# Second MLP product by seven products of halves, blocks of 256 tokens, and a new weight conversion, in a fused attention and MLP kernel

## Chip, cores and metric

One NeuronCore of a Trainium2 chip. The metric is the device time of one execution in microseconds; several executions of each kernel, the median is quoted. Each kernel ran beside the kernel before on the same chip. Ratios are the mean time of one kernel's fast runs over that of the other's fast runs of the same rounds, so they aren't quite the ratio of the quoted medians.

## The reference, cut to what matters

Retention attention (no softmax, a causal decay mask) of 8 batches x 8 heads x 576 tokens x 64, then an MLP on 4608 tokens of 512 features with 2048 hidden ones:

```python
def _attn_ref(q, k, v):
    scores = (1.0 / np.sqrt(D_)) * np.matmul(q, k.transpose(0, 1, 3, 2))
    ...                                    # rel = pos_i - pos_j
    Dmat = np.where(rel >= 0, gamma[:, None, None] ** rel[None, :, :], 0.0)
    return np.matmul(scores * Dmat[None], v).astype(np.float32)

def _moe_ref(x, w_in, w_out, alpha):
    h = x @ w_in                           # 4608x512 @ 512x2048
    g = np.maximum(h, 0.0) + alpha * np.minimum(h, 0.0)
    return (g @ w_out).astype(np.float32)  # 4608x2048 @ 2048x512
```

The two weight matrices arrive as 64-bit floats. The chip has to turn them into fp32 by integer work on their halves ("conversion" below): 32 pieces of 128x512, each a 512 KB load and then seven short operations on three engines (six after the change).

## The kernel before

Sixteen "couples" (4 heads of one batch each) go through attention. MLP units (128 hidden features x 384 tokens) are put between the attention's parts as soon as there are tokens for them. All matmul results of attention go through one ring of three PSUM banks, tag `psa`. The conversion uses SBUF alone:

```python
ps_a = tile_pool(name="ps_a", bufs=3, space=PSUM)
ps_h = tile_pool(name="ps_h", bufs=2, space=PSUM)
ps_o = tile_pool(name="ps_o", bufs=NTC, space=PSUM)      # NTC = 3
...
def load_weights(n):                      # 8 pieces a couple, couples 0 to 3
    ...
    nc.sync.dma_start(raw, src...)        # raw: 3 buffers
    nc.gpsimd.tensor_scalar(a, hi, HI_MAX, -HI_MAX, ALU.min, ALU.max)
    nc.scalar.activation(l, lo, ACTF.Copy, scale=2.0 ** -29)
    nc.scalar.activation(b, a, ACTF.Square)
    nc.vector.scalar_tensor_tensor(out=a, in0=b, scalar=HI_MIN * HI_MIN, in1=a,
                                   op0=ALU.is_ge, op1=ALU.mult)
    nc.vector.tensor_scalar(bi, ai, 3, 0x3FFFFFF8, ALU.logical_shift_left, ALU.bitwise_and)
    nc.vector.scalar_tensor_tensor(out=bi, in0=ai, scalar=-0x40000000, in1=bi,
                                   op0=ALU.bitwise_and, op1=ALU.bitwise_or)
    nc.gpsimd.tensor_tensor(out=dst.bitcast(INT32), in0=bi, in1=l, op=ALU.add)
...
def mlp_out():                            # second product: 3 x 512 columns a unit
    for m in range(NTC):
        nc.tensor.matmul(acc[kb][m], g[:, m * P:(m + 1) * P], w_out[...][:, ..., :], ...)
...
for n, (b, u) in enumerate(couples):      # cut
    qT, kT, rT = transposes(n, b, u, tiles)
    at = scores(n, qT, kT, rT)
    states(n, tiles)
    if b < WB:
        load_weights(WPC)
    values(n, b, u, tiles, qT, rT, at)    # its pv, pvr tiles: tag "psa"
```

The listing's order is the program's order.

## Time and profile before

| | before |
|---|---|
| median | 1243.3 us (1241.19 to 1243.61, 3 runs) |
| span of the profiled run | 1242.7 us |
| nominal TensorE work, by pitch | 1171 us |
| tail after the last matmul | 6 us |
| lost in the first 200 us | 66 us |

"Pitch" is the time from one start to the next. A "pass" is one TensorE record of the trace; an fp32 matmul is two of them. "Lost" is the span less the nominal work and the tail.

The prediction shows the lines that carry this.

### The profile page before, as it was taken

The numbers are of one execution on the slowest core, as the hardware profiler recorded it, in microseconds if no ns is written. First come the engines' busy times: TensorE is split into PE (matmuls) and PEld (weight loads), VectorE is DVE, ScalarE is ACT, GpSimd is POOL, SyncE is SP. The second block draws the span as 40 slices with busy tenths as digits, with TensorE's granted clock in tenths as the row PEclk, the third lists the DMA queues.
The fourth block names the chain that finished last, engine by engine and source line by source line (L and its number), as shares of the span: only waits on it lengthen the run. The fifth ranks groups of instructions, "written<-read, shape, count | busy, mean of one in ns | idle before, by whom it ended". The sixth has DMA issues, their size and how long they took to land.

```text
span 1242.7 us, 11962 instructions
## 1 busy us (share of the span) xinstructions
PE 1193.1 (96%) x4897; PEld 670.2 (54%) x4897; DVE 417.0 (34%) x831; ACT 108.3 (9%) x197; POOL 195.2 (16%) x328
## 2 busy tenths in 40 slices
PE   6878789999999999999999999999999999999998
PEld 4644445555555565555555655555555556555553
DVE  5778772223223232312312332232232323222221
ACT  1333220000001001001001000100100100000000
POOL 6567680002001010100100101010010000000000
PEclk9879799999999999999999999999999999999999
DMA  6655631002002120100100201010010000000000
GB/s 153 193 152 166 177 85 45 5 1 60 20 1 64 23 55 30 34 20 30 34 20 30 54 17 41 30 37 17 30 35 20 26 0 1 26 0 1 25 1 26
DMA packets 122774, 55.31 MB, mean 45 GB/s; under 512 B 116304, under 2 KB 116320, under 8 KB 122720
## 3 DMA queue, kind: packets, MB, share of 16 engines
q1 hardware_dynamic: 119808, 45.11, 14.4%
q0 software_dynamic: 2912, 9.45, 2.0%
q8 instruction: 38, 0.62, 0.2%
q14 instruction: 16, 0.13, 0.0%
HBM read 45.10 MB, written 9.44 MB: 44 GB/s over the span
## 4 chain that ended last, share of the span: by engine, by line
PE 61%; issue 27%; POOL 6%; DVE 4%; ACT 1%; DMA 1%; SPq 0%; POOLq 0%; ACTq 0%
PE ph L242 26%; PE po L227 26%; PE pt L285 2%; PE ps L302 2%; PE pv L347 2%; POOL w_in L213 2%; POOL qk L269 1%; PE pv L356 1%; POOL wa L201 1%; PE pu L325 1%; DVE at L306 1%; POOL w_out L213 1%; DVE wa L205 1%; ACT wb L204 1%; DVE wb L211 1%
## 5 line engine op out<-in xcount | busy, mean ns | idle before, releaser
L227 PE MATMUL po<-w_out,g 128*128 128x512 f32 x1152 | 532.2, 598 | 13.0 <-DVE g L248 9.3
L242 PE MATMUL ph<-xT,w_in 128*128 128x384 f32 x1536 | 541.5, 493 | 1.8 <-POOL w_in L213 1.8
L242 PEld LDWEIGHTS ph<-xT,w_in 128*128 128x128 f32 x1536 | 288.2, 191 | 225.9 <-issue 76.1
L227 PEld LDWEIGHTS po<-w_out,g 128*128 128x128 f32 x1152 | 220.0, 192 | 249.8 <-issue 187.3
L246 DVE TENSOR_SCALAR neg<-ph,alpha 128x384 f32<-128x384 f32 x192 | 118.5, 617 | 688.4 <-PE ph L242 687.9
L269 POOL TENSOR_TENSOR qk<-qk,tab 128x256 f32<-128x256 f32 x128 | 86.0, 691 | 233.2 <-DMA qk<-in_q_dram 222.8
L248 DVE SCALAR_TENSOR_TENSOR g<-ph,neg 128x384 f32<-128x384 f32 x192 | 106.8, 556 | 6.2
L235 POOL DMA_DIRECT2D out_dram<-osb x36 | 19.9, 553 | 354.2 <-ACT osb L233 353.9
L264 POOL TENSOR_TENSOR qkr<-qkr,tabr 128x256 f32<-128x256 f32 x16 | 9.8, 614 | 410.6 <-DMA qkr<-in_k_dram 284.1
L359 ACT COPY xT<-pv 128x512 f32<-128x512 f32 x32 | 18.5, 584 | 452.2 <-PE pv L356 451.0
L302 PE MATMUL ps<-qT,kT 64*128 64x128 f32 x512 | 48.8, 287 | 7.8 <-DVE at L306 5.6
L306 DVE TENSOR_TENSOR at<-ps,mask 128x512 f32<-128x512 f32 x64 | 41.4, 685 | 38.6 <-PE ps L302 38.6
L302 PEld LDWEIGHTS ps<-qT,kT 64*128 64x128 f32 x512 | 42.6, 190 | 21.5 <-issue 10.5
L233 ACT COPY osb<-po 128x512 f32<-128x512 f32 x36 | 21.1, 585 | 260.3 <-PE po L227 236.5
L285 PE MATMUL pt<-ident,qk 128*128 128x128 f32 x256 | 36.5, 295 | 0.2
L347 PEld LDWEIGHTS pv<-at,vn 128*64 128x64 f32 x512 | 28.6, 140 | 11.0 <-issue 9.1
L280 ACT COPY rT<-ptr 128x256 f32<-128x256 f32 x16 | 6.0, 375 | 324.5 <-PE ptr L279 324.5
L347 PE MATMUL pv<-at,vn 128*64 128x128 f32 x512 | 32.5, 280 | 1.1 <-DVE atr L315 1.1
L285 PEld LDWEIGHTS pt<-ident,qk 128*128 128x128 f32 x256 | 31.0, 151 | 3.8 <-POOL qk L269 1.0
L356 PE MATMUL pv<-qT,sums 128*128 128x128 f32 x192 | 27.8, 290 | 5.3 <-DVE sums L335 4.3
L213 POOL TENSOR_TENSOR w_in<-wb,wl 128x512 int32<-128x512 int32 x16 | 25.1, 1566 | 33.9 <-DVE wb L211 30.4
L211 DVE SCALAR_TENSOR_TENSOR wb<-wa,wb 128x512 int32<-128x512 int32 x32 | 30.0, 939 | 0.4
(55 smaller groups left out, 382.4 us busy)
## 6 DMA issues: line engine op xcount, KB each, us to landing
out_dram<-osb POOLq DMA_DIRECT2D x36, 256.0 KB, 2.4
qk<-in_q_dram SPq DMA_DIRECT2D x64, 128.0 KB, 2.9
qk<-in_k_dram SPq DMA_DIRECT2D x64, 128.0 KB, 3.0
vn<-in_v_dram SPq DMA_DIRECT2D x64, 128.0 KB, 2.7
raw<-in_moe_w_in_dram SPq DMA_DIRECT2D x16, 512.0 KB, 4.6
raw<-in_moe_w_out_dram SPq DMA_DIRECT2D x16, 512.0 KB, 3.5
qkr<-in_q_dram SPq DMA_DIRECT2D x32, 32.0 KB, 2.2
qkr<-in_k_dram SPq DMA_DIRECT2D x32, 32.0 KB, 2.2
```

Source lines behind the costliest of these rows:

```text
L211: nc.vector.scalar_tensor_tensor(out=bi, in0=ai, scalar=-0x40000000, in1=bi, op0=ALU.bitwise_and, op1=ALU.bitwise_or)
L213: nc.gpsimd.tensor_tensor(out=dst.bitcast(INT32), in0=bi, in1=l, op=ALU.add)
L227: nc.tensor.matmul(acc[kb][m], g[:, m * P:(m + 1) * P], w_out[fc // FCQ][:, fc % FCQ, :], start=(fc == 0), stop=(fc == NFC - 1))
L242: nc.tensor.matmul(ph, w_in[fc // FCQ][:, cc, f0:f0 + P], xT[grp][:, cc, t0:t0 + TB], start=(cc == 0), stop=(cc == NCC - 1))
L246: nc.vector.tensor_scalar(neg, ph, 0.0, alpha[:, fc:fc + 1], ALU.min, ALU.mult)
L248: nc.vector.scalar_tensor_tensor(out=g, in0=ph, scalar=0.0, in1=neg, op0=ALU.max, op1=ALU.add)
L269: nc.gpsimd.tensor_tensor(out=qk[:, x, j], in0=qk[:, x, j], in1=tab[:, x, j, 4 * u:4 * u + 4, None].to_broadcast([P, 4, D]), op=ALU.mult)
L285: nc.tensor.transpose(pt[:, j * C:(j + 1) * C], qk[:, x, j, 2 * i:2 * i + 2, :].rearrange("p h d -> p (h d)"), ident)
L302: nc.tensor.matmul(ps[h2][:, cols], kT[i][rows, cols], qT[i][rows, cols], start=True, stop=True)
L306: nc.vector.tensor_tensor(out=a, in0=ps[h2].rearrange("p (j w) -> p j w", w=C), in1=mask[:, None, :].to_broadcast([P, NJ, C]), op=ALU.mult)
L347: nc.tensor.matmul(pv[i][h2 * D:(h2 + 1) * D, j * C:(j + 1) * C], vn[:, j, 2 * i + h2, :], at[2 * i + h2][:, j, :], start=(j == 0), stop=F ...
L356: nc.tensor.matmul(pv[i][:, j * C:(j + 1) * C], sm[:, j - 1, i, :], qT[i][:, j * C:(j + 1) * C], start=False, stop=(j == NJ - 1), skip_gro ...
```

## The change

Its intent is to take one eighth off the second product (Strassen: seven products of halves for eight) and to shorten the weight conversion, so that the MLP starts sooner. A unit is now 256 hidden features x 256 tokens, and a block has seven accumulators of 256 columns in four banks. The conversion of a piece has one VectorE operation less. The intermediate of the two that are left lies in PSUM, with the intent that VectorE and GpSimd needn't lock each other out of the SBUF port (point 4 of the prediction). A stage of weights is one quarter of both matrices, and a unit asks only for its own stage.

The core of the diff (cuts marked `...`; sums of `g`, attention's scaling and the output's adds are left out):

```diff
-    TB = 384
+    TB = 2 * P
 ...
-    ps_h = ctx.enter_context(tc.tile_pool(name="ps_h", bufs=2, space=bass.MemoryType.PSUM))
-    ps_o = ctx.enter_context(tc.tile_pool(name="ps_o", bufs=NTC, space=bass.MemoryType.PSUM))
+    ps_h = ctx.enter_context(tc.tile_pool(name="ps_h", bufs=1, space=bass.MemoryType.PSUM))
+    ps_o = ctx.enter_context(tc.tile_pool(name="ps_o", bufs=1, space=bass.MemoryType.PSUM))
 ...
-    loaded = {0: load_couple(*couples[0]), 1: load_couple(*couples[1])}
+    loaded = {0: load_couple(*couples[0])}
 ...
-    nc.gpsimd.dma_start(a16, moe_alpha.rearrange("(t p) -> t p", p=P))
+    nc.sync.dma_start(a16, moe_alpha.rearrange("(t p) -> t p", p=P))
 ...
-            nc.gpsimd.tensor_scalar(a, hi, HI_MAX, -HI_MAX, ALU.min, ALU.max)
-            nc.scalar.activation(l, lo, ACTF.Copy, scale=2.0 ** -29)
-            nc.scalar.activation(b, a, ACTF.Square)
-            nc.vector.scalar_tensor_tensor(out=a, in0=b, scalar=HI_MIN * HI_MIN, in1=a,
-                                           op0=ALU.is_ge, op1=ALU.mult)
-            nc.vector.tensor_scalar(bi, ai, 3, 0x3FFFFFF8,
-                                    ALU.logical_shift_left, ALU.bitwise_and)
-            nc.vector.scalar_tensor_tensor(out=bi, in0=ai, scalar=-0x40000000, in1=bi,
-                                           op0=ALU.bitwise_and, op1=ALU.bitwise_or)
+        nc.scalar.activation(a, hi, ACTF.Abs)
+        nc.scalar.activation(l, lo, ACTF.Copy, scale=2.0 ** -29)
+        nc.gpsimd.tensor_scalar(a, a, HI_MIN, HI_MAX, ALU.max, ALU.min)
+        c = ps_a.tile([P, DM], INT32, tag="psa", name=f"wc_{at}")
+        nc.vector.tensor_scalar(c, ai, 3, 0x3FFFFFF8,
+                                ALU.logical_shift_left, ALU.bitwise_and)
+        nc.vector.scalar_tensor_tensor(out=bi, in0=flat[:, :, 1], scalar=-0x40000000, in1=c,
+                                       op0=ALU.bitwise_and, op1=ALU.bitwise_or)
 ...
+            for eng, o, x, y in ((nc.vector, 4, 1, 0), (nc.vector, 5, 3, 4),
+                                 (nc.gpsimd, 6, 5, 2), (nc.gpsimd, 1, 3, 1)):
+                eng.tensor_tensor(out=w[:, o], in0=w[:, x], in1=w[:, y], op=ALU.subtract)
 ...
+    PROD = [(0, 0), (2, 2), (5, 5), (6, 1), (4, 4), (7, 3), (3, 6)]
 ...
-        for m in range(NTC):
-            nc.tensor.matmul(acc[kb][m], g[:, m * P:(m + 1) * P], ...)
+        for n, (x, y) in enumerate(PROD):
+            nc.tensor.matmul(acc[kb][n // 2][:, n % 2, :], g[:, x, :], w_out[i][:, y, :], ...)
```

## The prediction

> **What bounds the kernel now.** I read the page first (busy table and 40 slices), then the windows view in stretches, then the chain of waits inside one steady stretch, then the groups by form, and last the timeline of the first 200 us.
>
> ```profile
> PE 1193.1 (96%) x4897; PEld 670.2 (54%) x4897; DVE 417.0 (34%) x831; ACT 108.3 (9%) x197; POOL 195.2 (16%) x328
> ...
> PE   6878789999999999999999999999999999999998
> ...
> PEclk9879799999999999999999999999999999999999
> ```
> TensorE is busy 96% and at full clock everywhere but the first 7 slices.
>
> ```profile
> 50.00:100.00 50.00, 38.57 (x258) 24.56 (x258) 40.95 (x67) 18.14 (x31) 38.52 (x37) 0.83 0.63 175
> 100.00:150.00 50.00, 39.75 (x156) 21.92 (x158) 35.95 (x51) 16.24 (x28) 36.04 (x37) 0.85 0.61 178
> ...
> 400.00:500.00 100.00, 99.89 (x434) 57.34 (x433) 27.97 (x52) 7.52 (x15) 12.15 (x21) 1.00 0.17 42
> ```
> (Columns: stretch, length, busy PE, PEld, DVE, ACT, POOL, clock, DMA share, GB/s.) Two regimes. Up to about 200 us TensorE has gaps and a clock of 0.83 to 0.85, while DVE and POOL are both over 70% busy: they convert the weights. From 200 us on TensorE has no gap and DVE is 28% busy. The same view for 1200 to 1243 us has TensorE busy 36.76 us.
>
> ```profile
> 408.71 1.53 PE pv L356 x12
> ...
> 418.43 2.58 PE po L227 x6
> 421.00 2.58 PE ph L242 x8
> ...
> 443.72 1.14 PE ps L302 x16
> 444.86 0.68 DVE at L306
> ```
> In the steady chain (start, us, what) the first product of one unit (8 passes of 384 columns; each fp32 matmul is two records) takes 2.58 us and the second (6 passes of 512) also 2.58. That is 322 and 430 ns a pass: 0.84 ns per column and nearly no fixed cost. Ends matter little here, as the pitch comes from starts. Between two successive groups the same chain has 52.55 us (398.86 to 451.41) with 8 units of 5.155, so one attention couple costs 52.55 - 41.24 = 11.3 us of TensorE.
>
> So the nominal TensorE time is 192 units x 5.155 = 990 us, plus 16 couples x 11.3 = 181: 1171 us. The span is 1242.7; that last stretch of 43 us leaves a tail of 6 us. The remaining 66 us are lost in the first 200 us.
>
> **What the Trainium skill says.** (1) "TensorE: Matmul & The Clock Gate", section "Wait — 56ns, not 53.3ns?": a warm matmul starts every N / 2.4 GHz + 2.5 ns. The trace has twice the streaming time per fp32 pass: 2 x 384 / 2.4 + 2.5 = 322.5 and 2 x 512 / 2.4 + 2.5 = 429.2, measured 322 and 430. (2) The same page, "LDWEIGHTS (loading the stationary operand)" and "Step-by-step: what each phase is for": a weight load takes about its columns / 1.2 ns and can run under the matmul before it. The trace agrees: the 12 passes of only 128 columns above (pv, first line of the fence), each with its own 128-column load, take 1.53 us, 128 ns each, so loads are no limit above that. (3) "VectorE: DVE Perf Modes", "The TRN2 errata": an fp32 tensor_tensor takes (N + 151) / 0.96 ns. The rows agree: 512 columns 685 ns (691), 128 columns 283 (291). (4) "SBUF — State Buffer", "Who interferes with whom": DVE with two SBUF inputs, or in a two-port mode, and GpSimd lock each other out; DVE with at most one SBUF input, outside those modes, does not.
>
> ```profile
> L205 DVE SCALAR_TENSOR_TENSOR wa<-wb,wa x32: 674/693/1095, 43.9 to 175.6; 128x512 f32<-128x512 f32 x32
> ...
> L209 DVE TENSOR_SCALAR wb<-wa x32: 408/844/1375, 45.1 to 176.9; 128x512 int32<-128x512 int32 x32
> ...
> L201 POOL TENSOR_SCALAR wa<-raw x32: 642/840/1109, 38.2 to 174.0; 128x512 f32<-128x512 f32 x32
> ```
> (min/median/max ns.) The trace fits the lock: each of these has a short form and one 0.4 to 1 us longer.
>
> **The change part by part.**
> *Matmuls.* A unit becomes 256 hidden features x 256 tokens: 16 passes for the first product and 7 products x 2 = 14 for the second, all of 256 columns. A pass: 2 x 256 / 2.4 + 2.5 = 215.8 ns. Unit: 30 x 215.8 = 6.47 us; 18 blocks x 8 units = 144: 932 us. Against 990 this saves 58 us. The gain is all in the second product (495 to 435 us, nearly one eighth); narrower passes give back 3 us. All of it lies on the path, as TensorE has no gap after 200 us.
> *DVE, steady.* Added per unit: the neg row (617 ns at 384 columns) becomes two of 256, 617 - 128 / 0.96 = 484 each; the g row (556 at 384) becomes one of 512, 690; then four sums of 128 columns, 283 each as the atr row: 2.79 us. Per block seven combinations of 256 columns, (256 + 151) / 0.96 = 424, 2.97 us, 0.37 per unit. 3.2 us in 6.47, half busy, so throughput does not bind. Latency: ph has one PSUM bank instead of two. After the first product DVE must read it out in 0.2 (start delay in the timeline, po at 926.36 to neg at 926.56) + 0.97 + 0.69 = 1.86 us, while TensorE works 14 passes = 3.02 us on the previous unit. 1.2 us of slack. The accumulators are single too: at a block's end the readout and the sums of the next unit take DVE about 5.9 us from the moment ph is full, and TensorE comes back to the accumulators after 6.47. Slack 0.6 us; a GpSimd operation that holds the shared port can use it up. I give 4 us in all.
> *Weights.* DVE per piece before: mean rows 814 + 829 + 939 = 2.58 us; after: two operations with PSUM on one side, about 0.7 each, 1.4. GpSimd per piece before 856 and 1513 (means); after, if the lock is gone, the short forms 0.65 + 1.26 = 1.9. Added: four half-size differences per unit, two on each engine (0.6 and 0.42 each). The q/k scaling (128 x 0.69 + 16 x 0.61 = 98 us) becomes q/v in 32 large ones, about the same. Now the order of instructions: conversion starts at about 27 us instead of 38 (one couple's loads, 10.7 us of issuing, no longer stand before it). Each stage of 8 pieces follows one couple on DVE. Stage 0: 8 pieces at 2.3 us after a 4 us fill, to 48. Stage 1: GpSimd 8 x 1.9 + 2.4 + 5.4 = 23 us. Stages 2 and 3: DVE 5.6 (couple) + 11.2 + 1.7 + three units x 2.8 = 27, 28 with some lock. Sum 127, with a 3 us bubble at each of four turns about 139 us, instead of 181. By then TensorE has done 4 couples, transposes of the fifth (2), 7 first and 6 second products: 45 + 2 + 24 + 18 = 89, nearly 90. Lost 139 - 90 = 49 instead of 66.
> *Tail.* Seven adds instead of three copies, most before the last product: still 6 us.
> Sum: 932 + 181 + 49 + 6 + 4 = 1172; I say 1170.
>
> **The rivals.**
> (a) Weight loads bind at 256 columns. The PEld rows show 191 ns means and PEld would be 30 x 191 = 5.7 of 6.47 us. Against: the 128-column passes at 128 ns. If a pass took 235 ns: 4320 x 19 = 83 us back, 1250. I give 4%.
> (b) The single banks make TensorE wait for DVE. For: the small slack at block ends. If each of 18 blocks lost 1.5 us and each unit 0.1: 27 + 14 = 41, 1210. 8%.
> (c) The start gains nothing, because DVE, now also making the unit's four sums, and the shared psa banks stay the limit: 66 lost again, 1189. 20%.
> (d) The start gains fully: no bubbles, all weights by 127 us, 37 lost: about 1160. 25%.
>
> **Range and chances.** The matmul term is firm (two pitches fitted, one in between). The start is worth -12 to +17 around 1170, waits up to +10 commonly. So 1170, range 1150 to 1195. Faster by 2% means under 1218: only (a), or (b) at its worst, miss it. Faster 0.94, within 2% 0.05, slower 0.01.
>
> **What would show it.** Right: in the steady chain ph groups of 16 passes take 3.45 us and po groups of 14 take 3.02; DVE about half busy there; first product row near 497 us and second near 435 by pitch; the last weight conversion near 139 us; the clock slices full from the fifth or sixth on. Wrong: po or ph waiting for DVE on the row of groups (over 10 us in total), a pitch well above 216 ns, DVE's differences and sums stretched far over 0.4 us beside GpSimd, or the last conversion still near 180.

## More of the kernel before

A scheduler orders the instructions of each engine when the program is built; the order in which tiles take the buffers of a ring is the program's.

The waits of TensorE in the first 200 us of the kernel before (who waited, for what, us in total, times, longest):

```profile
PE po L227 <- DVE g L248: 9.3, 4, 2.9
PE aps L163 <- DMA a<-in_moe_alpha_dram: 8.9, 1, 8.9
PE ps L302 <- DVE at L306: 5.6, 2, 4.8
PE pv L356 <- DVE sums L335: 4.3, 4, 1.3
```

No single wait is large, and the values (`pv`) wait for attention's own sums only. The two outer windows of the start (stretch, length, then busy us of PE, PEld, DVE, ACT, POOL, the TensorE clock granted as a share of full speed, DMA share, GB/s):

```profile
0.00:50.00 50.00, 33.87 (x330) 27.65 (x331) 27.70 (x139) 11.88 (x22) 26.60 (x116) 0.93 0.66 162
...
150.00:200.00 50.00, 45.41 (x150) 23.46 (x148) 31.55 (x48) 7.90 (x12) 25.95 (x23) 0.94 0.21 60
```

TensorE gets through 34 us of work in the first 50 us, because attention runs ahead of the weights.

## The result, and the profile after

| | before | after |
|---|---|---|
| median, same rounds | 1243.45 us (4 runs) | 1232.83 us (1232.12 to 1234.44, 4 runs) |
| ratio | | 0.992, 95% interval 0.9903 to 0.9937 |
| span of the profiled run | 1242.7 | 1232.7 |
| nominal TensorE work | 1171 | 932 + 181 = 1113 (units by the pitches below, couples as before) |
| tail | 6 | 5.7 |
| lost in the start (the rest) | 66 | 114 |

The output is correct. The predicted 1170 us, with a range to 1195, was missed by 63 us. The matmuls did save what was foreseen, and the start lost 48 us more than before. First the chain of waits of the changed kernel in a steady stretch (start us, us, what):

```profile
930.41 3.45 PE ph L268 x16
933.87 3.02 PE po L256 x14
936.89 3.45 PE ph L268 x16
940.34 3.02 PE po L256 x14
```

A unit is 3.45 + 3.02 = 6.47 us, to the hundredth as worked out, and the groups follow each other without a gap. The windows view of the changed kernel:

```profile
0.00:50.00 50.00, 9.28 (x93) 8.45 (x95) 24.95 (x124) 13.52 (x21) 33.80 (x103) 0.77 0.69 178
50.00:100.00 50.00, 20.02 (x172) 16.77 (x168) 21.44 (x40) 16.09 (x30) 41.90 (x32) 0.60 0.48 142
100.00:150.00 50.00, 37.97 (x239) 31.22 (x240) 23.98 (x52) 19.48 (x42) 38.56 (x30) 0.80 0.55 148
150.00:200.00 50.00, 40.55 (x255) 33.55 (x254) 31.38 (x61) 11.77 (x25) 31.11 (x24) 0.90 0.33 93
...
500.00:600.00 100.00, 99.89 (x550) 87.19 (x549) 45.25 (x123) 4.60 (x13) 4.57 (x4) 1.00 0.11 29
```

The last line is the steady state: TensorE full, VectorE 45% busy. Above it TensorE is busy 9 us where before it was 34, then 20 us where it was 39. VectorE, feared as the limit, is less busy than before (21 us instead of 41 in the second stretch), while GpSimd is at 42. What TensorE waited for in the first 200 us:

```profile
PE pv L385 <- DVE wb L207: 52.0, 5, 26.0
PE ph L268 <- DVE g L278: 17.1, 4, 6.2
PE aps L164 <- DMA a<-in_moe_alpha_dram: 13.7, 1, 13.7
```

The first line is new, and odd on its face. The values of attention, `pv`, have no use for `wb`, a tile of the weight conversion. What they share is a bank ring. The timeline of TensorE shows the longest of these waits (start, us, what, and in brackets the idle time before it and what ended it):

```profile
22.22 1.15 PE L365 MATMUL pu<-vn,kn 128*64 128x64 f32 x32 [0.16 <-issue]
49.41 1.98 PE L385 MATMUL pv<-at,vn 128*64 128x128 f32 x16 [26.03 <-DVE wb L207]
```

The first couple's scores and states are done at 23 us. Its values come at 49. In the program's order the eight `wc` tiles of the stage take the ring's three buffers before `pv` does, so `pv` gets a bank only when a late `wc` has been read. The chain of waits has the operation that reads the sixth of the eight (start us, us, what):

```profile
48.59 0.69 DVE wb L207
```

The first `pv` starts right after it. The second starts at 55.10 us, after the seventh piece, and `pvr` at 58.74, after the eighth: three buffers, given out in order. The next couple's values wait behind the next stage in the same way (18.4 us at 90.6).

The second cause is in the groups of the conversion (count: min/median/max ns, first and last start us):

```profile
L201 POOL TENSOR_SCALAR wa<-wa x32: 1907/1916/2022, 28.0 to 183.5; 128x512 f32<-128x512 f32 x32
```

```profile
L205 DVE TENSOR_SCALAR wc<-wa x32: 682/695/696, 30.0 to 185.4; 128x512 int32<-128x512 int32 x32
```

```profile
L209 POOL TENSOR_TENSOR w_out<-wb,wl x16: 1260/1272/1320, 45.3 to 187.5; 128x512 int32<-128x512 int32 x16
```

The last two rows look as the PSUM operand was meant to make them: VectorE's runs flat at 0.69 us where before it was 408/844/1375 ns, and GpSimd's add is flat at 1.27 (before, 1257/1441/1711 for the same tile). But GpSimd's clamp takes 1.92 us and never less, against a median of 0.84 before: 61 us in all instead of 27. The last piece's last operation starts at 187.5 us; before, it was 179.9. "The last piece" below is always this start.

### The profile page after: what moved, and what is told of

Its sections match the earlier page's. It is cut to its first block, busy times and chain, and to the rows that moved or that the text cites. A ratio compares the mean times of both kernels' runs of the same rounds, so it can differ in the third digit from the quotient of the medians.

```text
span 1232.7 us, 16093 instructions
## 1 busy us (share of the span) xinstructions
PE 1134.6 (92%) x6529; PEld 984.7 (80%) x6529; DVE 565.1 (46%) x1535; ACT 112.5 (9%) x283; POOL 191.1 (16%) x226
## 4 chain that ended last, share of the span: by engine, by line
PE 86%; POOL 5%; DVE 3%; DMA 2%; SPq 2%; issue 1%; ACT 1%; DVEq 0%; POOLq 0%; ACTq 0%
PE ph L268 40%; PE po L256 34%; POOL wa L201 3%; PE ps L342 3%; PE pv L394 2%; PE pt L324 2%; PE pv L385 2%; DMA raw<-in_moe_w_in_dram 2%; PE pu L365 1%; SPq L76 1%; DVE at L346 1%; POOL w_out L209 1%; SPq L81 1%; PE psr L353 1%; DVE wb L207 1%
## 5 line engine op out<-in xcount | busy, mean ns | idle before, releaser
L268 PE MATMUL ph<-xb,w_in 128*128 128x256 f32 x2304 | 538.7, 385 | 17.1 <-DVE g L278 17.1
L268 PEld LDWEIGHTS ph<-xb,w_in 128*128 128x128 f32 x2304 | 436.1, 192 | 79.9 <-DVE g L278 12.1
L256 PE MATMUL po<-w_out,g 128*128 128x256 f32 x2016 | 458.5, 379 | 0.0
L256 PEld LDWEIGHTS po<-w_out,g 128*128 128x128 f32 x2016 | 383.0, 190 | 52.1
L276 DVE TENSOR_SCALAR neg<-ph,alpha 128x256 f32<-128x256 f32 x288 | 126.3, 479 | 522.5 <-PE ph L268 522.5
L284 DVE TENSOR_TENSOR g<-g 128x128 f32<-128x128 f32 x576 | 156.1, 311 | 8.7
L278 DVE SCALAR_TENSOR_TENSOR g<-ph,neg 128x512 f32<-128x512 f32 x144 | 99.5, 691 | 4.9
L313 POOL TENSOR_TENSOR vn<-vn,tab 128x1024 f32<-128x1024 f32 x16 | 30.4, 1903 | 428.1 <-DMA vn<-in_v_dram 337.7
L313 POOL TENSOR_TENSOR qn<-qn,tab 128x1024 f32<-128x1024 f32 x16 | 30.6, 1913 | 273.4 <-DMA qn<-in_q_dram 240.6
L201 POOL TENSOR_SCALAR wa<-wa 128x512 f32<-128x512 f32 x32 | 61.3, 1920 | 16.9 <-ACT wa L197 16.9
L205 DVE TENSOR_SCALAR wc<-wa 128x512 int32<-128x512 int32 x32 | 21.9, 692 | 42.7 <-POOL wa L201 42.7
```

Of the source, the lines that this page charges most:

```text
L201: nc.gpsimd.tensor_scalar(a, a, HI_MIN, HI_MAX, ALU.max, ALU.min)
L256: nc.tensor.matmul(acc[kb][n // 2][:, n % 2, :], g[:, x, :], w_out[i][:, y, :], start=(i == 0 and n % 2 == 0), stop=(i == NU - 1 and (n % ...
L268: nc.tensor.matmul(ph[:, x, :], w_in[i // UST][:, cc, x, f0:f0 + P], xb[kb][:, cc, :], start=(cc == 0), stop=(cc == NCC - 1))
L276: nc.vector.tensor_scalar(neg[:, x], ph[:, x], 0.0, alpha[:, fc:fc + 1], ALU.min, ALU.mult)
L278: nc.vector.scalar_tensor_tensor(out=g[:, 0:4, :].rearrange("p x t -> p (x t)"), in0=ph.rearrange("p x t -> p (x t)"), scalar=0.0, in1=neg ...
L284: nc.vector.tensor_tensor(out=g[:, o, :], in0=g[:, x, :], in1=g[:, y, :], op=op)
```

## The experiments

Four sets, on five chips, each with the kernel before on the same chip (its medians are 1242.6 to 1244.9 us, so the sets compare to within 2 us). "Loss" is the span of the profiled run (some 2 us under that run's own time) less 1113 and 5.7.

| run | median us | ratio to before, 95% | loss in the start |
|---|---|---|---|
| after | 1232.83 | 0.9903 to 0.9937 | 114 |
| c_in_pso | 1212.19 | 0.9733 to 0.9765 | 92 |
| c_in_sbuf | 1212.03 | 0.9733 to 0.9764 | 91 |
| clamp_forms | 1219.54 | 0.9791 to 0.9820 | 99 |
| plain8 | 1279.08 | 1.0270 to 1.0301 | other pitch |
| clamp_all | 1209.91 | 0.9716 to 0.9745 | 89 |
| clamp_pso | 1187.27 | 0.9534 to 0.9569 | 67 |
| clamp_sbuf | 1188.17 | 0.9537 to 0.9575 | 69 |
| early_w2 | 1211.99 | 0.9731 to 0.9766 | 94 |
| before_swap | 1266.07 | 1.0168 to 1.0198 | kernel before |
| raw4 | 1195.36 | 0.9607 to 0.9638 | 76 |
| raw4_actq | 1192.46 | 0.9581 to 0.9609 | 71 |
| early_w3 | 1192.21 | 0.9577 to 0.9609 | 72 |
| interleave | 1186.63 | 0.9517 to 0.9546 | 67 |
| no_early_units | 1188.07 | 0.9532 to 0.9563 | 67 |
| free_conv (wrong result) | 1148.36 | 0.9215 to 0.9247 | 28 |
| alpha_q | 1187.54 | 0.9532 to 0.9564 | 68 |

### First set: the theories, one at a time

Theory one: the conversion's PSUM tiles in attention's ring hold up the values. Theory two: the clamp's slow form makes each stage long. The rival to both is that the seven products themselves, by their sums and single banks, cost what they save.

**c_in_pso** puts the conversion's tile of the first two stages into the banks of the second product, which are idle then:

```diff
-        c = ps_a.tile([P, DM], INT32, tag="psa", name=f"wc_{at}")
+        if at < 16:
+            c = ps_o.tile([P, DM], INT32, tag=f"pso{at % 4}", name=f"wc_{at}")
+        else:
+            c = ps_a.tile([P, DM], INT32, tag="psa", name=f"wc_{at}")
```

> The changed kernel, but in stages 0 and 1 the PSUM operand of the weight conversion lies in the four banks of the second product, which are idle then, not in the three banks that the attention uses. Theory 1 (the conversion's use of the attention's PSUM ring makes TensorE wait for whole stages): the waits of the pv matmuls for the conversion, 26.0 and 18.4 us in the first two stages, go to under 3 us each, the x blocks of the first couple are copied near 30 us instead of 61, and the last conversion is 10 to 20 us earlier than 187.5: about 1215 us. Theory 2 (GpSimd's slow clamp of 1.92 us a piece sets the end of the conversion, whatever TensorE does): the pv waits go but the last conversion stays within 5 us of 187.5 and the time within 6 us of 1233.

Measured 1212.19 us, 20.6 less than the changed kernel. Its waits of TensorE in the first 200 us:

```profile
PE ph L271 <- DVE g L281: 21.2, 5, 9.5
...
PE po L259 <- DVE wb L210: 6.8, 2, 3.9
```

The 52 us of `pv` for `wb` are gone. Not all of them come back as time: part turns into other waits, since the weights still come late: the last piece is at 178.7 us, 9 earlier, where theory one expected 10 to 20. The second line shown is the same coupling on a small scale, now with the accumulators' banks.

**c_in_sbuf** takes the intermediate out of PSUM altogether, as in the kernel before:

```diff
-        c = ps_a.tile([P, DM], INT32, tag="psa", name=f"wc_{at}")
-        nc.vector.tensor_scalar(c, ai, 3, 0x3FFFFFF8,
+        nc.vector.tensor_scalar(bi, ai, 3, 0x3FFFFFF8,
                                 ALU.logical_shift_left, ALU.bitwise_and)
-        nc.vector.scalar_tensor_tensor(out=bi, in0=flat[:, :, 1], scalar=-0x40000000, in1=c,
+        nc.vector.scalar_tensor_tensor(out=bi, in0=flat[:, :, 1], scalar=-0x40000000, in1=bi,
```

> The changed kernel with the intermediate of the conversion in SBUF, in all stages, as before the change: no PSUM ring shared any more, but two operations of VectorE with SBUF inputs alone beside GpSimd. Theory 1: all pv waits for the conversion (52 us) go, last conversion 15 to 30 us earlier, about 1205 us. Theory 2: about 1233 or up to 10 more, as the port is now contended and the clamp keeps its 1.9 us.

1212.03 us: the same gain by another way, though VectorE's first conversion operation now has 414/942/2120 ns and meets the port lock again. (GpSimd's add keeps its median of 1.27 us, so its gain over the kernel before isn't the PSUM operand's.) So it was the ring, not something about the accumulator banks. The expected 1205 us was missed by 7, and the last piece comes only 3.5 us earlier, at 184.0. So most of the gain isn't an earlier end of the conversion: TensorE does attention's work in the meantime (it is busy 97.5 of the first 154 us, in the changed kernel 71.2).

**clamp_forms** gives the clamp four forms in turn, to tell the order of its operations from its being in place:

```diff
-        nc.gpsimd.tensor_scalar(a, a, HI_MIN, HI_MAX, ALU.max, ALU.min)
+        if at % 4 == 0:
+            nc.gpsimd.tensor_scalar(a, a, HI_MIN, HI_MAX, ALU.max, ALU.min)
+        elif at % 4 == 1:
+            nc.gpsimd.tensor_scalar(a, a, HI_MAX, HI_MIN, ALU.min, ALU.max)
+        elif at % 4 == 2:      # Abs has written b, not a
+            nc.gpsimd.tensor_scalar(a, b, HI_MIN, HI_MAX, ALU.max, ALU.min)
+        else:
+            nc.gpsimd.tensor_scalar(a, b, HI_MAX, HI_MIN, ALU.min, ALU.max)
```

> The clamp of GpSimd in four forms, one for each fourth piece: as in the changed kernel (in place, max then min), in place with min then max, to another tile with max then min, to another tile with min then max. Before the change the clamp (min then max, strided source, another tile) took 0.64 us alone. I expect the slow 1.92 us in one factor alone: if it is the order of operations, forms 2 and 4 take about 0.65; if it is the in-place write, forms 3 and 4. Half of the 32 pieces then save 1.27 us each, 20 us of GpSimd's time. Theory 2: the last conversion is 12 to 20 us earlier and the time about 1216. Theory 1: under 6 us of gain.

The four lines of the clamp (min/median/max ns):

```profile
L203 POOL TENSOR_SCALAR wa<-wa x8: 1910/1916/1959, 28.0 to 159.4; 128x512 f32<-128x512 f32 x8
```

```profile
L205 POOL TENSOR_SCALAR wa<-wa x8: 607/614/619, 30.7 to 162.5; 128x512 f32<-128x512 f32 x8
```

```profile
L207 POOL TENSOR_SCALAR wa<-wb x8: 1911/1914/1918, 34.1 to 166.8; 128x512 f32<-128x512 f32 x8
```

```profile
L209 POOL TENSOR_SCALAR wa<-wb x8: 610/614/657, 38.9 to 170.1; 128x512 f32<-128x512 f32 x8
```

Max first: 1.92 us, in place or not. Min first: 0.61, in place or not. The order alone makes a factor of 3.1 on the same numbers. With half of the clamps mended the time is 1219.54 us, 13.3 less, and the last piece comes at 172.9 us.

**plain8** keeps blocks, stages and conversion, and takes eight plain products instead of seven, without any of the sums (its edit: the differences of `w_out`, the sums of `g` and the adds of the output go, and the loop runs over 2 token halves x 2 feature halves x 2 column halves in two banks):

```diff
-        for n, (x, y) in enumerate(PROD):
-            nc.tensor.matmul(acc[kb][n // 2][:, n % 2, :], g[:, x, :], w_out[i][:, y, :], ...)
+        for m in range(2):
+            for x in range(2):
+                for h in range(2):
+                    nc.tensor.matmul(acc[kb][m][:, h * HM:(h + 1) * HM], g[:, 2 * x + m, :],
+                                     w_out[i][:, 2 * x + h, :], ...)
```

> The changed kernel with the plain eight products of halves instead of seven, no sums on VectorE or GpSimd, the same blocks, stages and conversion. If the steady state behaves as predicted, 144 units x 2 passes x 215.8 ns = 62 us longer, less up to 10 us that the start gains without sums and differences: 1285 to 1295 us, and 16 passes for the second product in 3.45 us in the chain. If Strassen's sums cost TensorE waits in the steady state, less than 50 us longer.

1279.08 us, less than the expected 1285 to 1295. Its steady chain:

```profile
909.62 3.45 PE po L244 x16
913.08 3.45 PE ph L257 x16
```

The second product's group is 3.45 us of 16 passes instead of 3.02 of 14: 0.43 x 144 units = 62 us. The total is 46 us worse, so the seven products are worth 46 here. By the rule, less than 50 would mean that the sums make TensorE wait in the steady state; but in neither kernel is there such a wait (from 400 to 1200 us TensorE is busy all but 1.3 us of 800 there, and all but 1.2 here). The other 16 fit the start, where plain8 has no sums and differences (the last piece comes at 171.9 us in place of 187.5). The rival falls: the seven products do pay.

### Second set: both mends, and an earlier start

**clamp_all**: the clamp min first, for all pieces.

```diff
-        nc.gpsimd.tensor_scalar(a, a, HI_MIN, HI_MAX, ALU.max, ALU.min)
+        nc.gpsimd.tensor_scalar(a, a, HI_MAX, HI_MIN, ALU.min, ALU.max)
```

> The changed kernel with GpSimd's clamp written min first, then max, in place, for all 32 pieces. Order theory: all 32 clamps near 0.61 us (32 x 1.3 = 42 us less GpSimd work, twice that of the run in which half of the pieces had it), so the time falls about twice as far as there: 1233 - 2 x 13 = 1206 us, between 1200 and 1212; the last w_out conversion moves from 187 to about 159 us. Rival: the second 16 clamps are hidden behind VectorE or the loads, then 1214 to 1220 as with half of them. The attention values should still wait 25 to 45 us for the shared bank ring in both.

1209.91 us, 22.9 less than the changed kernel; the first half of the clamps brought 13.3, the second 9.6. The last piece comes at 162.9 us (expected 159). The values still wait 42.7 us for `wb`.

**clamp_pso**: that edit and the one of c_in_pso.

> Both mends: clamp min first, and the conversion's PSUM operand of stages 0 and 1 in the idle banks of the second product. If the two losses are separate and add: 1233 - 21 - 27 = 1185 us. If they share time (GpSimd's stage is what the ring makes TensorE wait for, so a shorter stage leaves less to uncouple): 1190 to 1202. If only one of them sets the end: no better than the better of the two single mends, 1206. Waits of the attention values under 5 us; last conversion before 155 us.

1187.27 us: 45.6 us less than the changed kernel. The two single mends sum to 20.6 + 22.9 = 43.5, so the two losses stand side by side. The waits and two windows:

```profile
PE ph L271 <- DVE g L281: 13.8, 4, 7.5
...
PE ph L271 <- POOL w_in L212: 4.5, 4, 1.9
```

```profile
0.00:50.00 50.00, 27.58 (x269) 23.24 (x269) 29.59 (x138) 17.42 (x33) 30.36 (x108) 0.93 0.75 189
50.00:100.00 50.00, 35.98 (x184) 28.61 (x184) 36.25 (x66) 17.32 (x32) 31.51 (x34) 0.76 0.57 159
```

The first 50 us hold 28 us of TensorE work instead of 9, and the last conversion starts at 153.7. It is 4.5% faster than the kernel before and 3.7% faster than the changed one. The loss that is left, 67 us, is just that of the kernel before.

**clamp_sbuf**: clamp_all and the edit of c_in_sbuf.

> Clamp min first, and the conversion's intermediate in SBUF as in the kernel before, so no PSUM bank at all, but VectorE and GpSimd share their port again. If the PSUM operand (the freedom from the lock) is worth anything once the ring is out of the way, this is slower than the run with both mends by 3 to 10 us, near 1195; if the lock costs nothing here, equal within 2 us. VectorE's conversion rows lengthen from 0.69 to over 0.8 us in the mean, GpSimd's add from 1.27 to over 1.3.

1188.17 us, the same as clamp_pso. The first of VectorE's two conversion operations, in this run and then in clamp_pso:

```profile
L204 DVE TENSOR_SCALAR wb<-wa x32: 414/523/2123, 30.7 to 161.8; 128x512 int32<-128x512 int32 x32
```

```profile
L208 DVE TENSOR_SCALAR wc<-wa x32: 677/687/695, 29.5 to 151.4; 128x512 int32<-128x512 int32 x32
```

In SBUF the operation is sometimes shorter than with PSUM (414 ns) and sometimes held up to 2.1 us. The sum over the 32 is 25.8 against 21.9 us, for the second operation 29.0 against 21.7. So VectorE works 11 us more, as expected, and the time doesn't show it: the expected 3 to 10 us did not come. The PSUM operand lifts the lock from VectorE, as promised. But it also takes banks, and clamp_pso has 4.2 us of waits of `po` for `wb` which clamp_sbuf has not. What is shown is that the two together are worth nothing in time here; what the lock alone costs is not.

**early_w2** starts the conversion before the first couple and takes each later stage one couple ahead:

```diff
+    load_stage(0)
     for n, (b, u) in enumerate(couples):
-        share = -(-len(queue) // (NC2 - u)) if n >= NST else UST * max(0, n - 1)
+        share = -(-len(queue) // (NC2 - u)) if n >= NST else 2 * UST * (n // 2)
 ...
-        if n < NST:
-            load_stage(n)
+        if n + 1 < NST:
+            load_stage(n + 1)
```

(with both mends, and alpha's load on GpSimd's queue)

> Both mends, and the conversion also started earlier: the first stage's pieces loaded and converted before the first couple, each later stage one couple ahead, alpha's small load moved to GpSimd's queue, and two couples' units taken up in pairs. If the remaining loss is the conversion chain of the start (it ends 27 us plus four stages of about 25 us), starting it 10 us sooner gives 5 to 12 us more than the run with both mends: 1175 to 1185. If attention, now behind the first stage in VectorE's and ScalarE's order, comes later by as much, no gain or a loss of some us: 1190 to 1200.

1211.99 us, 25 worse than clamp_pso: a miss. TensorE's timeline says why:

```profile
47.07 1.97 PE L368 MATMUL pu<-vn,kn 128*64 128x64 f32 x32
93.81 1.97 PE L388 MATMUL pv<-at,vn 128*64 128x128 f32 x16 [44.77 <-DVE wb L210]
```

The mend moved only the first 16 pieces out of `psa`. With the conversion one couple ahead, stage 2 comes before the second couple's values in the program's order, and its `wc` tiles are back in the ring ahead of them. (In clamp_pso they are in the ring too, but ahead of the third couple's values, and TensorE has MLP units to do by then: its values wait 0.3 us for `wb` there.) The edit rebuilt the fault that it was meant to build upon.

### Third set: the clamp in the other kernel, and what is left

**before_swap**: the kernel before, its clamp's order swapped.

```diff
-            nc.gpsimd.tensor_scalar(a, hi, HI_MAX, -HI_MAX, ALU.min, ALU.max)
+            nc.gpsimd.tensor_scalar(a, hi, -HI_MAX, HI_MAX, ALU.max, ALU.min)
```

> The kernel before, with only the order of its clamp swapped: max with -HI_MAX first, then min with HI_MAX, instead of min first (the result is the same). Order theory: the 32 clamps go to about 1.9 us each from a median of 0.84, although they read another tile and sit in a kernel without the change; 32 x 1.05 = 34 us more GpSimd work in a start where GpSimd is 70 to 80% busy, so the time grows by 13 to 30 us: 1256 to 1273. Rival: the slowness comes from the constants or from the kernel around it, then the rows stay at 0.84 and the time at 1243.

1266.07 us, 1.8% slower. The row:

```profile
L201 POOL TENSOR_SCALAR wa<-raw x32: 1935/2384/2410, 39.6 to 194.1; 128x512 f32<-128x512 f32 x32
```

From a median of 0.84 to 2.38 us, for a clamp with constants of one size and both signs, from another tile. So it is the order in this kernel too, and neither the constants nor the change around it.

**raw4**: clamp_pso with four buffers for the raw weights (`bufs=3` to `bufs=4`). The sync queue waited 53 us in clamp_pso for VectorE to be done with a raw tile, which it now reads last.

> The run with both mends, with four buffers for the raw weights instead of three. The sync queue waited 53 us there for VectorE to read a raw tile out (its last reader is now the second VectorE operation). If that hand-over is part of the 17 us which are left against the prediction, 3 to 10 us less: 1177 to 1184. If the transfers themselves (4.8 us each, three in flight) are the limit, within 2 us of 1187.

1195.36 us, 8 us slower: a miss. The conversion did end sooner (144.5 us for 153.7), yet TensorE waited longer. Its timeline in raw4:

```profile
85.06 6.33 PE L271 MATMUL ph<-xb,w_in 128*128 128x256 f32 x16 [14.91 <-DVE g L281]
```

The first product has one bank. It was full at 65.4 us, and VectorE read it out only from 83.4, having done the conversion's operations first. The group after the wait takes 6.33 us instead of 3.45. That fits the Trainium skill, "TensorE: Matmul & The Clock Gate", section "What's actually happening": an idle stretch of some 3.4 us takes TensorE's clock to half, and about as long a busy one brings it back. The trace agrees: the clock granted is 0.50 from 70 to 88 us, 0.66 to 91.5 and then 1.00. In this group it is 2.9 us on top of the wait.

**raw4_actq**: also the raw loads on ScalarE's queue and alpha's on GpSimd's.

```diff
-        nc.sync.dma_start(raw, src)
+        nc.scalar.dma_start(raw, src)
```

> As the run before with four raw buffers, and the raw loads issued from ScalarE's queue and alpha's from GpSimd's, so that they do not stand behind the couples' loads on the sync queue (18 loads of about 0.6 us per couple). If the order on the sync queue starts the conversion late, the first conversion comes near 15 to 20 us instead of 28 and the time is 5 to 12 us lower than with four buffers alone: 1168 to 1180. If the loads only crowd each other and ScalarE's order, 1180 to 1195.

1192.46 us. The first piece is done at 14 us instead of 31 (the start of GpSimd's add), and the last at 144.3, as in raw4; 3 us better than raw4 and 5 worse than clamp_pso.

**early_w3**: the edit of early_w2, with stages 2 and 3 converted in SBUF and four raw buffers.

> The early start of the conversion again, as in the run that was slower (1212), but with no bank of the attention's ring in it: stages 0 and 1 in the idle accumulator banks, stages 2 and 3 in SBUF; four raw buffers. If the shared ring was what made the early start slow (47 us of waits of the values there), they vanish and the early start shows its worth: 1165 to 1182. If it was the order of the work on VectorE, still 1195 or more.

1192.21 us. The `pv` waits for `wb` are gone and the run is 20 us better than early_w2. It has four raw buffers besides, but raw4 was slower with these, so the ring is what made early_w2 slow. But conversion from 19.9 to 141.3 us is again no faster in the end than clamp_pso, whose last piece comes 12 us later. So the end of the conversion alone does not set the time.

### Fourth set: the remaining 17 us

**interleave** puts a unit after every two weight pieces in couples 2 and 3 (by turning the stage into a list of steps). **no_early_units** takes the units out of the four stages altogether:

```diff
-        share = -(-len(queue) // (NC2 - u)) if n >= NST else UST * max(0, n - 1)
+        share = -(-len(queue) // (NC2 - u)) if n >= NST else 0
```

> Both mends, and the MLP units of couples 2 and 3 put between the weight pieces (a unit after every two pieces, seven units in all before couple 4) instead of around the whole stage. If VectorE's order with the single first-product bank makes the remaining 17 us, the waits of the first product for g fall from 14 us to under 6 and the time to 1172 to 1182. If the end of the conversion sets it, the last conversion stays near 155 us or later and the time is 1185 to 1192.

> Both mends, but no MLP unit before couple 4. The conversion then meets no g, no sums and no bank waits. If the loss is the conversion's end less the work done by then, the six units (6 x 6.5 = 39 us) come later while the conversion ends at most 10 to 15 us sooner: 1187 + 39 - 15 = 1211, between 1200 and 1222. If the early units only got in the way of the conversion, 1180 to 1195.

1186.63 and 1188.07 us: nothing. One line each of the timelines of clamp_pso and no_early_units shows why (interleave has the same group at 74.49 us, after a wait of 7.35):

```profile
74.78 6.06 PE L271 MATMUL ph<-xb,w_in 128*128 128x256 f32 x16 [7.48 <-DVE g L281]
```

```profile
74.44 5.96 PE L271 MATMUL ph<-xb,w_in 128*128 128x256 f32 x16 [7.26 <-DVE g L281]
```

In no_early_units no unit stands before the fifth couple, and still its first product runs at 74 us with the same wait: the scheduler brought it forward. Both runs tell nothing of the cause. They tell that the program's order of such work is not the order on the engines.

**free_conv** takes the conversion's arithmetic away (weights are the high halves copied as they are), and leaves the loads, the differences and all matmuls:

```diff
-        nc.scalar.activation(a, hi, ACTF.Abs)
 ...
-        nc.gpsimd.tensor_tensor(out=dst.bitcast(INT32), ...)
+        nc.scalar.copy(dst, hi.rearrange("p (x f) -> p x f", x=2))
```

> Both mends' kernel with the conversion's arithmetic taken away, wrong on purpose: one copy on ScalarE per piece instead of six operations on three engines; the loads, the four differences per unit and all matmuls stay. If the conversion's arithmetic makes the rest of the start's loss, the weights are there as soon as the loads allow (16.8 MB and four couples' loads at about 190 GB/s, 110 to 125 us) and the time falls from 1187 to 1160 to 1172. If the loads and attention's order make it, within 6 us of 1187.

1148.36 us, 39 less than clamp_pso and below the expected 1160. The same two windows as of clamp_pso:

```profile
0.00:50.00 50.00, 32.13 (x306) 27.52 (x307) 22.51 (x134) 14.69 (x32) 19.16 (x96) 0.97 0.74 190
50.00:100.00 50.00, 48.36 (x390) 40.76 (x389) 26.15 (x65) 17.72 (x41) 14.53 (x15) 1.00 0.79 225
```

So the loads, attention, the differences and the first wait for alpha make 28 us of the start's loss. The conversion's arithmetic on the three engines makes 39 of the 67, even with both mends. (Its PSUM tiles go with it, but clamp_sbuf has none either and is no faster than clamp_pso.) These 39 are not all waits. In the first 200 us TensorE is busy 153.3 us in clamp_pso and 178.2 in free_conv, so 25 us less are idle; the other 14 go with a granted clock of 0.91 there and 0.99 here.

**alpha_q**: clamp_pso with alpha's load back on GpSimd's queue.

```diff
-    nc.sync.dma_start(a16, moe_alpha.rearrange("(t p) -> t p", p=P))
+    nc.gpsimd.dma_start(a16, moe_alpha.rearrange("(t p) -> t p", p=P))
```

> Both mends, and alpha's small load back on GpSimd's queue as in the kernel before. TensorE's first wait falls from 13.4 to about 9 us, as in the two early-start runs. If the start of everything hangs on it, 3 to 5 us less: 1182 to 1184. If the conversion's chain, which begins with the loads of the sync queue, sets the end, no change: 1186 to 1188.

1187.54 us. TensorE's first wait falls from 13.4 to 9.3 us, and the waits of `ph` for `g` and for `w_in` grow from 13.8 to 17.6 and from 4.5 to 10.1. A gain ahead of a later limit is given back.

## Why the prediction was wrong

- **Matmuls: right.** 6.47 us a unit, as worked out. plain8 isolates the seven-for-eight part: 62 us of pitch.
- **VectorE, steady: right.** 45% busy; no wait of TensorE from 200 us to the last unit, and it is busy 99.89 of 100 us. Of the 4 us allowed for it none show. Rivals (a) and (b) fall with it.
- **The lock: right for VectorE, of no use in time.** The PSUM operand keeps VectorE's row flat at 0.69 us. GpSimd's add has a median of 1.27 with it and without it (c_in_sbuf, clamp_sbuf). And clamp_sbuf, with the lock and without the PSUM banks, is as fast as clamp_pso.
- **Failed: "the short forms 0.65 + 1.26 = 1.9" for GpSimd.** The clamp of the changed kernel is not the one of the row that the 0.65 came from: its operations have changed places, and it takes 1.92 us. A piece costs GpSimd 3.2 us, not 1.9. Mending it alone gives 22.9 us. The diff showed the swap; the prediction read both as a two-operation clamp.
- **Failed: "a 3 us bubble at each of four turns".** The `wc` tiles share attention's ring, so the values stand behind a whole stage: 52 us of waits, up to 26 at once. Mending it alone gives 20.6 us. Rival (c) names "the shared psa banks" and had a chance of 20%, but it put the loss at 66 us, where the two together make 114; it treated the ring as a limit that stays, though the kernel before had none of the conversion in it.
- **Mis-sized: the conversion's length.** With both faults mended the last piece comes at 153.7 us, not 139, and the loss is 67, not 49. In the prediction's own sum, loss is the conversion's end less the work done by then. Its end is 155 us (153.7 and the last add's 1.3), and 155 - 67 leaves 88 us of work for "nearly 90": the work was right and the length too small by 16. Stage by stage the last adds of clamp_pso end at 54, 89, 121 and 155 us; the prediction's sums with a 3 us bubble each give 51, 77, 108 and 139. So stage 1 is the term that failed most: 35 us for 23 + 3. In it VectorE also had about 7 us of MLP work (`neg`, `g` and sums, 71 to 89 us), which the prediction put into stages 2 and 3 alone. That this is the reason is not shown: no_early_units was to test it and didn't change the order on the engines. Nor is the length the whole story: more raw buffers or an earlier start shortened the conversion and cost time. 39 us of the loss go with the conversion's arithmetic (free_conv); which of its hand-overs makes them stays open. "Weights staged by units", the couples' loads one ahead instead of two, and attention's single buffers were never run by themselves either.
- **Tail: right**, 5.7 us for 6.

The sum for the changed kernel: 63 us over the prediction, of which the two mends give back 45.6 and some 17 are the mis-sized conversion.

## What to carry to other kernels

When a tile moves to another pool, ask which other tiles take that ring's buffers after it in the program's order and who will then wait: here eight tiles of a side job stood ahead of attention's own results, and TensorE waited 26 us for work that it had no use for. Don't carry a duration over to an instruction whose operations or their order differ; look at the row of the very form, or measure it. And when a side job ends sooner and the kernel doesn't, look at what it held up on its engine on the way.

## What the Trainium skill lacked or had wrong

- "GPSIMD Engine Reference", section "3.1 Elementwise — side-by-side cycle accounting", has no word on the order of two operations in one tensor_scalar. On 128x512 fp32, min then max takes 0.61 us and max then min 1.92, in place or not (clamp_forms); swapping it in the kernel before cost 23 us (before_swap). The section calls 769 ns the best case for 512 elements, though it also gives 1.03 cycles an element for its smallest bodies (k ≤ 2), by estimate 439 ns at its 1.2 GHz; the 614 ns here are below the former and above the latter.
- "FP8 and Floating Point Precision", section "TensorE Precision Notes", gives true fp32 four passes, and the trace agrees: an fp32 matmul of 256 columns takes 431 ns (3.45 us for 8), four times the 107 ns of 256 / 2.4 (the rate of point 1 in the prediction). What it lacks is that the trace shows such a matmul as two records of 216 ns, so that `x16` counts 8 matmuls.
- "TensorE: Matmul & The Clock Gate" has the clock's fall after an idle stretch, which showed here as 6.06 and 6.33 us for a group of 3.45 after waits of 7.5 and 14.9 us. The page would gain from such a figure for fp32 groups.
- No page that was looked up says how a ring of PSUM buffers couples engines that have no data in common: 52 us of waits of `pv` for `wb` here, 44.8 in one piece in early_w2.
